# Gated linear attention with a soft mixture of experts on one core: output in 256 and 128 columns, the second expert weights by row halves, one unit in halves

## The chip, the cores and the metric

The kernel runs on one core of a Trainium2 chip. The metric is the device time of one execution in microseconds (us). All data are float32.

## The reference

A gated linear attention runs over 768 steps in 4 × 8 heads of 48 channels. Its output, laid out as x with 3072 rows of 384 columns, goes through a soft mixture of experts: 32 slots, four for each of 8 experts.

```python
f = 1.0 / (1.0 + np.exp(-f_logit))
for t in range(S):
    state = f[:, :, t, :, None] * state + np.einsum('bhd,bhe->bhde', k[:, :, t], v[:, :, t])
    y[:, :, t] = np.einsum('bhd,bhde->bhe', q[:, :, t], state)
...
logits = x @ phi
d = softmax of logits over the rows;  slot_input = d.T @ x
h = np.maximum(slot_input[e] @ w1[e], 0.0);  slot_out[e] = h @ w2[e]
c = softmax of logits over the 32 slots;  out = c @ slot_out
```

The two softmax lines and the two products behind them are written short here; the reference spells them out.

## The kernel before

The sequence is cut into chunks of 128 steps. Twelve units (u = 0 to 11) hold one chunk of two batches each: sixteen heads in eight pairs, 128 partitions by 1024 columns. Pairs 0 to 3 lie in columns 0 to 511, pairs 4 to 7 in the other half.

For each unit ScalarE (ACT) takes exponentials and logarithms of the gates (`d_exp`, `d_ln`), VectorE (DVE) scans them (`d_scan`, L194), ACT forms decay factors (`d_p`, L197, and `d_g`, L203), and GpSimd (POOL) multiplies q and k by them (`d_q`, L211, and `d_k`, L207). TensorE (PE) then computes `scores(u, w)` (L231) for w = 0 (pairs 0 to 3) and w = 1. DVE masks each half (`s_mask`, L240), and since both halves use one PSUM tile, PE may write half 1 only when half 0 is masked. `kt`, `inter`, `kv` and `intra` follow on PE. Units 0 to 2 are processed in two halves of 512 columns each at the start; all others as whole units.

Six groups g of two units each go through the router: logits (`c_lg`), a running maximum over the rows (`c_max`), exponentials (`c_exp`), transposes (`c_tr`, `c_copy`) and a running sum of slot inputs (`c_pin`, `c_join`). `c_max` and `c_join` contain DVE operations on one column (L329, L359).

The order on every engine is that of `at(t, ...)`: each call gets a due time, from a table `OFF` with T = 8.6 for one unit, and the calls are emitted sorted by it. An engine works its instructions off in that order.

After unit 11 comes a list written by hand (`last`, then `tail`). `up` multiplies slot inputs by w1, `turn` transposes the result, `down(h, j, kk)` multiplies by w2 and makes output half h of 192 columns, in 16 steps (j = 0, 1 and kk = 0 to 7). `slot_out` and `slot_out2` scale and spread the sum, `c_soft` and `c_soft2` are the softmax over the slots, `c_ct` transposes its result, and `combine(h, y)` (L486) makes a third y of half h. Copies by ACT (L488) and DVE (L490) put it into a stage in SBUF, and `store` (L493) sends it out: six stores of 768 KB.

All w1 tiles have a home of their own in `wr`. The 16 tiles of w2 (768 KB each, `load_w2`) use space that has been freed: nine go into regions of the arena, the other seven into places of w1 tiles that `up(0, 0)` and `up(0, 1)` have used. A tile holds one expert's 1024 rows by 192 columns, so `down(0, ...)` needs tiles 0 to 7 alone, and the seven late ones are for `down(1, ...)`.

Of the kernel before, what the change touches and what calls it, by code (L numbers as in the profile page):

```python
# [15 lines left out]
L = 128  # L16
NU = 12
# [5 lines left out]
NP = B * H // 2  # L23
NH = 2
HC = DM // NH
# [32 lines left out]
def gla_soft_moe_kernel(ctx: ExitStack, tc: tile.TileContext, q, k, f, v, vd, phi, w1, w2, out):  # L58
# [94 lines left out]
    def warm(n, t=None):  # L153

        for _ in range(n):
            nc.tensor.matmul(PC[:, 1, 384:512] if t is None else t, ones, ones, start=True, stop=True)  # L156

    def consts_1():

        for g in range(4):  # L160
            gs = slice(32 * g, 32 * g + 32)
            nc.vector.tensor_copy(same[gs].rearrange("p (h s) -> p h s", h=4), ident[gs, gs].unsqueeze(1).broadcast_to([32, 4, 32]))

        nc.gpsimd.memset(emask, 0.0)
        for e in range(NE):
            c = 32 * (e // 2) + 4 * e
            nc.gpsimd.memset(emask[:, e % 2, c : c + 4], 1.0)

# [198 lines left out]
    W2 = [(h, 2 * qq + j) for h in range(NH) for j in range(2) for qq in range(4)]  # L367
# [41 lines left out]
    DOWN = [PD[:, 0, :HC], PB[0][:, :HC]]  # L409
    SUM = [PD[:, 1, 256 : 256 + HC], PA[0][:, 256 : 256 + HC]]  # L410
# [13 lines left out]
    def t_zs():  # L424
        nc.vector.tensor_tensor(zs, wb, sms[:, 0:1], op=ALU.mult)
# [8 lines left out]
    ls = el[:, :, 1].rearrange("p v (n s) -> p v n s", n=4)  # L434
    cmv = cm.rearrange("p (v n) -> p v n", v=NV)

    def c_soft():
        cb = cmv.unsqueeze(3).broadcast_to([128, NV, 4, NS])
        nc.vector.tensor_reduce(cmv, ls, axis=AX.X, op=ALU.max)
        nc.vector.tensor_tensor(ls, ls, cb, op=ALU.subtract)  # L440
        nc.scalar.activation(el[:, :, 1], el[:, :, 1], AF.Exp)

    def c_soft2():
        cb = cmv.unsqueeze(3).broadcast_to([128, NV, 4, NS])
        nc.vector.tensor_reduce(cmv, ls, axis=AX.X, op=ALU.add)
        nc.vector.tensor_scalar(cm, cm, 1e-9, None, op0=ALU.add)
        nc.vector.reciprocal(cm, cm)
        nc.vector.tensor_tensor(ls, ls, cb, op=ALU.mult)
# [25 lines left out]
    FIN = [[(PC, PA[0], PA[1]), (PD, PB[1], PA[0]), (PC, PA[1], PB[1])], [(PC, PA[1], PB[1]), (PD, PA[0], PB[0]), (PC, PA[1], PB[1])]]  # L474
    stage = [wr[:, 7 + 3 * h : 10 + 3 * h].rearrange("p a (n d) -> p (a n) d", d=HC).rearrange("p (v n) d -> p v n d", n=4) for h in range(NH)]

    def combine(h, y):

        hs_ = slice(HC * h, HC * h + HC)
        two, b2, b3 = FIN[h][y]  # L480
        banks = [two[:, 0], two[:, 1], b2, b3]
        for n2 in range(2):
            for x in range(2):
                for n in (n2, n2 + 2):
                    ns = slice(32 * n, 32 * n + 32)
# [86 lines left out]
    early = {(1, "kv"): T + 6.0, (3, "scan"): 2 * T + 1.08, (3, "p"): 2 * T + 2.9, (3, "dq"): 2 * T + 2.95}  # L572
# [168 lines left out]
```

## Time and profile before

| | |
|---|---|
| median of 3 runs | 164.55 us (164.38 to 164.94) |
| the profiled execution | 164.74 us, span 163.0 us from first to last instruction |
| mean granted TensorE clock | 0.966 of full speed |
| busy: PE, DVE, ACT, POOL | 143.0, 112.6, 92.6, 53.4 us |
| HBM read, written | 48.82 MB, 4.72 MB |

All times of rows are in us from the start of the span. A row of the timeline has start, duration, engine, line, operation, tiles (out<-in), shape and count; in brackets, if the engine was idle before it, for how long and what released it. A row of the windows has the stretch, its length, busy time and instruction count of PE, PE's weight loads, DVE, ACT and POOL, then the granted TensorE clock (1.00 is 2.4 GHz, 0.50 is 1.2 GHz), the share of the DMA engines' time, and GB/s. The page's slices cut the span into 40 stretches of some 4.1 us and give tenths.

### The profile page before, as it was taken

The page shows a single profiled execution, that of the slowest core. Times are in us where ns is not written, and L with a number is a line of the kernel's source. Part 1 is how long each engine was busy: PE and PEld are TensorE (multiplying, and loading weights), DVE is VectorE, ACT ScalarE, POOL GpSimd, SP SyncE. Part 2 cuts the span into 40 slices and gives each one's busy share as a digit, 9 for nine tenths or more (in the row PEclk, how much of TensorE's full clock was granted, in tenths as well). Part 3 has the DMA queues.
Part 4 walks back from the last instruction along what each step waited for, and adds up shares of the span by engine and source line. Part 5 has one row for each costly group of instructions (what it writes and reads, how often), then busy time and mean ns, then how long its engine had stood idle before and what let it go on. Part 6 is the DMA issues. An engine that isn't in the chain of part 4 may idle for free.

```text
span 163.0 us, 5511 instructions
## 1 busy us (share of the span) xinstructions
PE 143.0 (88%) x2408; PEld 113.6 (70%) x2408; DVE 112.6 (69%) x152; ACT 92.6 (57%) x173; POOL 53.4 (33%) x41
## 2 busy tenths in 40 slices
PE   7998899959999998999989997999989998997500
PEld 7996798949979888798868885867523366664400
DVE  6879998787889979897989888763522708153700
ACT  4977997958778695859596786232302310232500
POOL 2006492665547191908383464600000000000000
PEclk9999999986999999999999999999999999999955
DMA  5999999999999999998999919999947996048690
GB/s 168 286 418 409 409 413 410 405 411 411 400 406 383 385 333 370 410 331 302 339 355 360 339 28 360 414 427 413 417 187 274 414 424 253 0 168 329 261 401 21
DMA packets 13136, 53.97 MB, mean 331 GB/s; under 512 B 1456, under 2 KB 1584, under 8 KB 13104
## 3 DMA queue, kind: packets, MB, share of 16 engines
q1 hardware_dynamic: 13104, 53.55, 84.8%
q8 instruction: 20, 0.33, 0.8%
q14 instruction: 12, 0.10, 0.2%
HBM read 48.82 MB, written 4.72 MB: 328 GB/s over the span
## 4 chain that ended last, share of the span: by engine, by line


## 5 line engine op out<-in xcount | busy, mean ns | idle before, releaser
L211 POOL TENSOR_TENSOR arena<-arena 128x1024 f32<-128x1024 f32 (+1 forms) x11 | 25.0, 2270 | 50.5 <-ACT arena L197 36.1
L240 DVE TENSOR_TENSOR arena<-pd,mask 128x1024 f32<-128x1024 f32 x23 | 27.9, 1213 | 8.7 <-PE pd L231 8.7
L194 DVE TENSOR_TENSOR_SCAN arena<-again,arena 128x1024 f32<-128x1024 f32 (+1 forms) x15 | 30.4, 2036 | 1.7 <-ACT arena L189 1.5
L231 PE MATMUL pd<-arena 48*128 48x128 f32 x368 | 26.7, 285 | 5.2 <-DVE arena L240 3.1
L231 PEld LDWEIGHTS pd<-arena 48*128 48x128 f32 x368 | 22.3, 187 | 9.9 <-DVE arena L240 5.2
L207 POOL TENSOR_TENSOR arena<-arena 128x1024 f32<-128x1024 f32 (+1 forms) x13 | 27.3, 2104 | 0.0
L284 PE MATMUL pb<-arena 128*48 128x128 f32 x384 | 23.5, 274 | 0.8 <-DVE arena L194 0.8
L197 ACT ACTIVATE arena<-arena 128x1024 f32<-128x1024 f32 (+1 forms) x15 | 13.3, 885 | 15.1 <-DVE arena L194 15.1
L284 PEld LDWEIGHTS pb<-arena 128*48 128x48 f32 x384 | 20.4, 123 | 1.5 <-DVE arena L194 1.0
L295 ACT COPY arena<-pb 128x512 f32<-128x512 f32 x24 | 13.5, 586 | 6.5 <-PE pb L284 6.2
L186 ACT ACTIVATE arena<-arena 128x1024 f32<-128x1024 f32 (+1 forms) x15 | 13.3, 887 | 1.7 <-DMA arena<-in_f_dram 1.7
L189 ACT ACTIVATE arena<-arena 128x1024 f32<-128x1024 f32 (+1 forms) x15 | 13.3, 887 | 0.5
L203 ACT ACTIVATE arena<-arena 128x1024 f32<-128x1024 f32 (+1 forms) x15 | 13.4, 893 | 0.3
L300 PE MATMUL pa<-ident,arena 112*128 112x112 f32 x96 | 12.3, 273 | 0.0
L275 PE MATMUL pb<-arena 48*48 48x128 f32 x320 | 10.9, 274 | 0.0
L300 PEld LDWEIGHTS pa<-ident,arena 112*128 112x128 f32 x96 | 10.4, 149 | 0.6 <-issue 0.2
L220 PE MATMUL pc<-ident,arena 112*128 112x112 f32 x80 | 10.6, 280 | 0.0
L156 PE MATMUL pd<-ones 128*128 128x128 f32 x64 | 9.6, 320 | 1.1 <-POOL ones L143 1.1
L156 PEld LDWEIGHTS pd<-ones 128*128 128x128 f32 x64 | 9.2, 233 | 1.2 <-POOL ones L143 1.1
L275 PEld LDWEIGHTS pb<-arena 48*48 48x48 f32 x320 | 8.4, 119 | 2.1 <-issue 1.6
L220 PEld LDWEIGHTS pc<-ident,arena 112*128 112x128 f32 x80 | 8.4, 149 | 1.2
L253 PE MATMUL pc<-arena 128*48 128x48 f32 x320 | 9.2, 210 | 0.0
(137 smaller groups left out, 208.9 us busy)
## 6 DMA issues: line engine op xcount, KB each, us to landing
wr<-in_w_dram SPq DMA_DIRECT2D x23, 768.0 KB, 8.6
arena<-in_w_dram SPq DMA_DIRECT2D x9, 768.0 KB, 9.0
arena<-in_q_dram SPq DMA_DIRECT2D x11, 512.0 KB, 7.5
arena<-in_k_dram SPq DMA_DIRECT2D x11, 512.0 KB, 6.3
arena<-in_f_dram SPq DMA_DIRECT2D x10, 512.0 KB, 7.4
arena<-in_v_dram SPq DMA_DIRECT2D x12, 384.0 KB, 7.1
out_dram<-wr SPq DMA_DIRECT2D x6, 768.0 KB, 3.5
arena<-in_f_dram SPq DMA_DIRECT2D x4, 256.0 KB, 4.0
```

The lines of the kernel that those rows point to most:

```text
L156: nc.tensor.matmul(PC[:, 1, 384:512] if t is None else t, ones, ones, start=True, stop=True)
L194: nc.vector.tensor_tensor_scan(t, cols(again, h), t, 0.0, op0=ALU.mult, op1=ALU.add)
L203: nc.scalar.activation(cols(G(u), h), cols(R("f", u), h), AF.Exp)
L207: (eng or nc.gpsimd).tensor_tensor(t, t, cols(G(u), h), op=ALU.mult)
L211: (eng or nc.gpsimd).tensor_tensor(t, t, cols(R("p", u), h), op=ALU.mult)
L220: nc.tensor.transpose(PC[:, a // 4, 128 * (a % 4) : 128 * (a % 4) + W], kq[:W, a], ident[:W, :W])
L231: nc.tensor.matmul(t[:, 128 * p : 128 * p + 128], kq[rs, 4 * w + p], qq[rs, 4 * w + p], start=True, stop=True)
L240: nc.vector.tensor_tensor(dst, src, mask.unsqueeze(1).broadcast_to(list(dst.shape)), op=ALU.mult)
L275: nc.tensor.matmul(ys[a][o : o + D], heads(S0(u), D)[rs, a], qq[rs, a], start=p == 0, stop=False, skip_group_check=True,)
L284: nc.tensor.matmul(ys[4 * w + p][o : o + D], vb(u, 4 * w + p, r ^ w), sc[:, r, p], start=u < 2 and p == 0, stop=p == 3, skip_group_check=True,
L295: nc.scalar.copy(xTs[u][:, w].rearrange("p a t -> p (a t)"), PB[w])
L300: nc.tensor.transpose(PA[w][:, 128 * p : 128 * p + W], xTs[u][:W, w, p], ident[:W, :W])
```

## The change

Output: instead of two halves of 192 columns there is a part of 256 and a part of 128 (`WC`, `CO`), each stored in three pieces (1024 KB and 512 KB). The tiles of w2 hold 512 rows by all 384 columns, so that both parts use every tile; a tenth tile gets a home in the region `xT`, and six are left for w1's places. Unit 3's `d_scan`, `d_p`, `d_g`, `d_q` and `d_k` run in halves. The softmax over the slots is done by halves of three groups: the first during units 10 and 11, the second in the tail, earlier than before; its two `c_ct` move ahead of the second half of `down(0, ...)`. Three one-column operations become `tensor_scalar` with a scalar per partition. The constants `same` and `emask` are made by POOL at the start instead of by DVE and POOL at 3 T. In `last`, the transposes of unit 11 are split around `c_lg`, and a `warm` gives its place to `c_ct(0)`.

```diff
+WC, CO = (256, 128), (0, 256)
...
-            nc.vector.tensor_tensor(nm(g), nm(g - 1), bmx, op=ALU.min)
+            nc.vector.tensor_scalar(nm(g), bmx, nm(g - 1), None, op0=ALU.min)
...
-            nc.vector.scalar_tensor_tensor(sms[:, 0:1], sms[:, 0:1], alpha, sms[:, 1:2], op0=ALU.mult, op1=ALU.add)
+            nc.vector.tensor_scalar(sms[:, 0:1], sms[:, 0:1], alpha, sms[:, 1:2], op0=ALU.mult, op1=ALU.add)
...
-    W2 = [(h, 2 * qq + j) for h in range(NH) for j in range(2) for qq in range(4)]
+    W2 = [(2 * qq + j, kh) for j in range(2) for kh in range(2) for qq in range(4)]
...
-        t = PA[1] if h else PC[:, 0]
+        t = PA[1] if h else PB[0]
...
-                DOWN[h][32 * qq : 32 * qq + 32], hT[:, j, kk, 32 * qq : 32 * qq + 32], w2u[h, 2 * qq + j][:, kk],
+                DOWN[h][32 * qq : 32 * qq + 32], hT[:, j, kk, 32 * qq : 32 * qq + 32], w2u[2 * qq + j, kk // 4][:, kk % 4, CO[h] : CO[h] + WC[h]],
...
-        items += [(up, 1, 0), (turn, 0, 1), (t_z,), (flag_2,), (up, 1, 1)]
+        items += [(up, 1, 0), (turn, 0, 1), (t_z,), (flag_2,), (c_soft2, 1), (up, 1, 1)]
...
-        items += [(turn, 1, 0), (turn, 1, 1), (c_soft2,)]
-        for x in range(8, 16):
-            items.append((down, 0, *STEPS[x]))
-        items += [(slot_out, 0), (c_ct, 0), (c_ct, 1)]
-        items += [(down, 1, *STEPS[x]) for x in range(2)]
+        items += [(turn, 1, 0), (turn, 1, 1), (c_ct, 1)]
+        items += [(down, 0, *STEPS[x]) for x in range(8, 16)]
+        items += [(slot_out, 0)]
+        items += [(down, 1, *STEPS[x]) for x in range(3)]
         items += [(slot_out2, 0)]
-        items += [(down, 1, *STEPS[x]) for x in range(2, 6)]
+        items += [(down, 1, *STEPS[x]) for x in range(3, 7)]
         for y in range(3):
             items += [(combine, 0, y), (store, 0, y)]
-            items += [(down, 1, *STEPS[x]) for x in ((6, 7, 8, 9), (10, 11, 12, 13), (14, 15))[y]]
+            items += [(down, 1, *STEPS[x]) for x in ((7, 8, 9), (10, 11, 12), (13, 14, 15))[y]]
...
+        (T + 1.08, d_scan, 3, 0), (T + 1.09, d_scan, 3, 1), (T + 2.9, d_p, 3, 0), (T + 2.91, d_g, 3, 0), (T + 2.92, d_q, 3, 0), (T + 2.93, d_k, 3, 0),
+        (T + 2.95, d_p, 3, 1), (T + 2.96, d_g, 3, 1), (T + 2.97, d_q, 3, 1), (T + 2.98, d_k, 3, 1),
...
-    at(3 * T, consts_1)
     at((NU - 1) * T + 6.5, flag)
+    at((NU - 2) * T + 6.45, c_soft, 0)
+    at((NU - 1) * T + 6.4, c_soft2, 0)
...
+    spare = span("xT")[0]
+    homes.append((None, spare))
     late = [(i, wr[:, i - len(homes)]) for i in range(len(homes), 16)]
...
-        (c_lg, NV - 1), (x_tr, NU - 1), (c_max, NV - 1), (c_exp, NV - 1, (0,)), (t_max,), (c_tr, NV - 1, (0,)),
-        (c_copy, NV - 1, (0,)), (x_copy, NU - 1), (t_max2,), (warm, 1), (c_pin, NV - 1), (c_join, NV - 1), (warm, 1),
+        (x_tr, NU - 1, (0,)), (c_lg, NV - 1), (x_tr, NU - 1, (1,)), (load_w2, len(homes) - 1, spare), (x_copy, NU - 1, (0,)), (c_max, NV - 1),
+        (c_exp, NV - 1, (0,)), (x_copy, NU - 1, (1,)), (t_max,), (c_tr, NV - 1, (0,)), (c_copy, NV - 1, (0,)), (t_max2,), (c_ct, 0),
+        (c_pin, NV - 1), (c_join, NV - 1), (warm, 1),
```

## Rows read from the trace of the kernel before

**Rows 1.** The page's 40 slices: DVE, POOL and the granted TensorE clock.
```profile
DVE  6879998787889979897989888763522708153700
POOL 2006492665547191908383464600000000000000
PEclk9999999986999999999999999999999999999955
```

**Rows 2.** Timeline of PE, scores of units 3, 7, 8 and 10.
```profile
34.74 1.16 PE L231 MATMUL pd<-arena 48*128 48x128 f32 x16 [1.83 <-POOL arena L207]
...
39.37 1.16 PE L231 MATMUL pd<-arena 48*128 48x128 f32 x16
...
74.05 1.16 PE L231 MATMUL pd<-arena 48*128 48x128 f32 x16 [0.19 <-DVE arena L240]
...
82.14 1.16 PE L231 MATMUL pd<-arena 48*128 48x128 f32 x16 [0.42 <-DVE arena L240]
...
99.86 1.16 PE L231 MATMUL pd<-arena 48*128 48x128 f32 x16 [1.18 <-DVE arena L240]
```

**Rows 3.** Windows: two stretches around the scores of unit 3.
```profile
32.92:34.74 1.82, 0.00 (x0) 0.00 (x0) 1.40 (x1) 1.80 (x6) 1.82 (x2) 1.00 1.05 423
...
35.92:39.20 3.28, 3.28 (x18) 3.19 (x18) 2.99 (x7) 1.97 (x3) 0.83 (x1) 0.50 1.03 412
```

**Rows 4.** Timelines of DVE, ACT and POOL, 19.8 to 38.9 us.
```profile
20.29 1.21 DVE L194 TENSOR_TENSOR_SCAN arena<-again,arena 128x512 f32<-128x512 f32 x1
...
26.49 2.28 DVE L194 TENSOR_TENSOR_SCAN arena<-again,arena 128x1024 f32<-128x1024 f32 x1
...
33.34 3.49 DVE L194 TENSOR_TENSOR_SCAN arena<-again,arena 128x1024 f32<-128x1024 f32 x1 [0.97 <-ACT arena L189]
36.76 0.89 DVE L162 COPY same<-ident 32x128 f32<-32x128 f32 x4
37.68 1.22 DVE L240 TENSOR_TENSOR arena<-pd,mask 128x1024 f32<-128x1024 f32 x1
...
19.79 0.62 ACT L197 ACTIVATE arena<-arena 128x512 f32<-128x512 f32 x1
...
20.49 2.08 POOL L211 TENSOR_TENSOR arena<-arena 128x512 f32<-128x512 f32 x1 [2.33 <-ACT arena L197]
...
32.33 2.36 POOL L207 TENSOR_TENSOR arena<-arena 128x1024 f32<-128x1024 f32 x1
```

**Rows 5.** Timelines of DVE and POOL in unit 6.
```profile
66.77 0.60 DVE L358 SCALAR_TENSOR_TENSOR pin<-pin,small,pa 128x384 f32<-128x384 f32 x1
67.30 1.93 DVE L359 SCALAR_TENSOR_TENSOR sms<-sms,small 128x1 f32<-128x1 f32 x1
...
66.83 2.38 POOL L207 TENSOR_TENSOR arena<-arena 128x1024 f32<-128x1024 f32 x1
```

**Rows 6.** Timeline of the tail, from the second half of `down(0, ...)`.
```profile
135.72 2.81 PE L458 MATMUL pd<-arena 128*32 128x192 f32 x64 [0.41 <-DVE arena L422]
138.72 0.55 PE L453 MATMUL pc<-ident,el 128*128 128x128 f32 x3 [0.19 <-DVE el L448]
...
142.27 0.42 PE L486 MATMUL pc<-s,ct 32*128 32x192 f32 x1
...
143.24 1.02 DVE L490 COPY wr<-pa 128x384 f32<-128x384 f32 x2 [4.17 <-PE pa L486]
...
144.33 0.35 SPq L493 DMA_DIRECT2D out_dram<-wr  x1
```

**Rows 7.** Windows: end of the late loads, and the stores.
```profile
136.50:137.50 1.00, 1.00 (x32) 0.81 (x28) 0.93 (x3) 0.00 (x0) 0.00 (x0) 1.00 0.43 158
...
145.05:147.00 1.95, 1.95 (x48) 1.23 (x42) 1.02 (x2) 0.80 (x1) 0.00 (x0) 1.00 0.98 403
...
151.75:153.05 1.30, 1.09 (x22) 0.77 (x16) 1.30 (x4) 1.06 (x2) 0.00 (x0) 1.00 0.08 19
...
153.05:159.00 5.95, 0.18 (x5) 0.00 (x0) 1.10 (x3) 0.80 (x1) 0.00 (x0) 0.69 0.98 391
```

More of the change, by code (lines that the diff above doesn't have):

```diff
@@ L23 @@
 NP = B * H // 2
+WC, CO = (256, 128), (0, 256)
 NH = 2
-HC = DM // NH
 UN = 1536
@@ L151, in consts_0 @@
             nc.vector.memset(PB[w], 0.0)
[L153 to L158, printed above, removed]
         for g in range(4):
             gs = slice(32 * g, 32 * g + 32)
-            nc.vector.tensor_copy(same[gs].rearrange("p (h s) -> p h s", h=4), ident[gs, gs].unsqueeze(1).broadcast_to([32, 4, 32]))
+            nc.gpsimd.tensor_copy(same[gs].rearrange("p (h s) -> p h s", h=4), ident[gs, gs].unsqueeze(1).broadcast_to([32, 4, 32]))
         nc.gpsimd.memset(emask, 0.0)
@@ L167, in consts_1, with warm @@
             nc.gpsimd.memset(emask[:, e % 2, c : c + 4], 1.0)
+    def warm(n, t=None):
+        for _ in range(n):
+            nc.tensor.matmul(PC[:, 1, 384:512] if t is None else t, ones, ones, start=True, stop=True)
     def cols(t, h):
@@ L295, in y_copy, with x_tr @@
             nc.scalar.copy(xTs[u][:, w].rearrange("p a t -> p (a t)"), PB[w])
-    def x_tr(u):
-        for w in range(2):
+    def x_tr(u, which=(0, 1)):
+        for w in which:
             for p in range(4):
@@ L424, in t_zs @@
     def t_zs():
-        nc.vector.tensor_tensor(zs, wb, sms[:, 0:1], op=ALU.mult)
+        nc.vector.tensor_scalar(zs, wb, sms[:, 0:1], None, op0=ALU.mult)
     def t_z():
@@ L431, in t_z, with ls, c_soft, c_soft2 @@
         nc.vector.reciprocal(rzs, rzs)
[L434 to L448, printed above, removed]
+    def ls(h):
+        c = cm[:, 12 * h : 12 * h + 12].rearrange("p (v n) -> p v n", v=3)
+        return el[:, 3 * h : 3 * h + 3, 1].rearrange("p v (n s) -> p v n s", n=4), c, c.unsqueeze(3).broadcast_to([128, 3, 4, NS])
+    def c_soft(h):
+        l, c, cb = ls(h)
+        nc.vector.tensor_reduce(c, l, axis=AX.X, op=ALU.max)
+        nc.vector.tensor_tensor(l, l, cb, op=ALU.subtract)
+        nc.scalar.activation(el[:, 3 * h : 3 * h + 3, 1], el[:, 3 * h : 3 * h + 3, 1], AF.Exp)
+    def c_soft2(h):
+        l, c, cb = ls(h)
+        nc.vector.tensor_reduce(c, l, axis=AX.X, op=ALU.add)
+        nc.vector.tensor_scalar(c, c, 1e-9, None, op0=ALU.add)
+        nc.vector.reciprocal(c, c)
+        nc.vector.tensor_tensor(l, l, cb, op=ALU.mult)
     def c_ct(h):
-        t = PA[1] if h else PC[:, 0]
+        t = PA[1] if h else PB[0]
         for x in range(3):
@@ L485, in combine @@
                     ns = slice(32 * n, 32 * n + 32)
-                    nc.tensor.matmul(banks[n][:, HC * x : HC * x + HC], ct[ns, 2 * y + x], s4[ns, hs_], start=True, stop=True)
+                    nc.tensor.matmul(banks[n][:, wc * x : wc * x + wc], ct[ns, 2 * y + x], s4[ns, hs_], start=True, stop=True)
         dst = stage[h][:, 2 * y : 2 * y + 2]
-        nc.scalar.copy(dst[:, :, :2].rearrange("p v n d -> p n v d"), two[:, :, : 2 * HC].rearrange("p n (v d) -> p n v d", v=2))
+        nc.scalar.copy(dst[:, :, :2].rearrange("p v n d -> p n v d"), two[:, :, : 2 * wc].rearrange("p n (v d) -> p n v d", v=2))
         for n in (2, 3):
-            nc.vector.tensor_copy(dst[:, :, n], banks[n][:, : 2 * HC].rearrange("p (v d) -> p v d", v=2))
+            nc.vector.tensor_copy(dst[:, :, n], banks[n][:, : 2 * wc].rearrange("p (v d) -> p v d", v=2))
     def store(h, y):
-        nc.sync.dma_start(out[h][:, 8 * y : 8 * y + 8], stage[h][:, 2 * y : 2 * y + 2].rearrange("p v n d -> p (v n) d"))
+        o, n = 4 * NV * CO[h], 8 * WC[h]
+        nc.sync.dma_start(out[:, o + n * y : o + n * y + n], stage[h][:, 2 * y : 2 * y + 2].rearrange("p v n d -> p (v n d)"))
     gok, gbad = P([128, 2], "gok"), P([1, 1], "gbad", I32)
@@ L582, in gla_soft_moe_kernel @@
         ):
-            if u < 2 and key in done or u == 2 and key in done and key != "pend" or u < 1 and key in done0 or u > NU - 3 and key in ("kt", "ktok", "kv", "st", "s2"):
+            if u < 2 and key in done or u == 2 and key in done and key != "pend" or u == 3 and key in ("scan", "p", "g", "dq", "dk") or u < 1 and key in done0 or u > NU - 3 and key in ("kt", "ktok", "kv", "st", "s2"):
                 continue
@@ L737 @@
     got = r.results[0]["out_0_dram"]
-    got = got.reshape(NH, L, NV, 2, 2, HC).transpose(3, 4, 2, 1, 0, 5).reshape(B * S, DM)
+    got = _np.concatenate([
+        got[:, 4 * NV * o : 4 * NV * (o + n)].reshape(L, NV, 2, 2, n) for o, n in zip(CO, WC)
+    ], axis=-1).transpose(2, 3, 1, 0, 4).reshape(B * S, DM)
     return _np.ascontiguousarray(got)
```

34 lines of the change are left out of this document (19 added, 15 removed).

## The prediction

> **What bounds the kernel now.** I first read the page's slices [rows 1]: the TensorE clock stands at full speed from the start to the end of the computation but for two slices, near 33 to 41 us. So PE does steady work, and it stops once. The timeline of PE shows where [rows 2]: scores(3, 0) start at 34.74 after a wait of 1.83 on POOL. The windows around it [rows 3] show PE at 0.00 busy from 32.92 to 34.74, and then, from 35.92 to 39.20, busy throughout at clock 0.50, the lower of its two levels (1.2 GHz). After that PE waits only now and then, 0.19 to 1.18 us, on masks by DVE [rows 2]. From 20 to 112 us the kernel is therefore a loop PE to DVE to ACT to POOL to PE with PE nearly full, and what makes a unit earlier moves all behind it. The last part has another limit. In its windows [rows 7] the first store's data moves at 403 GB/s, then there is a hole (19 GB/s from 151.75 to 153.05), and the last three stores run at 391 GB/s until 159.0, long after the engines have stopped. So the end is set by when the first store starts and by holes between stores. I read the tail's timeline for that [rows 6].
>
> **Unit 3 in halves.** Now POOL makes q and k of the whole unit, the second product from 32.33 to 34.69, and PE waits for it although scores(3, 0) read only columns 0 to 511 [rows 2, 4]. The scan's first half takes 1.21 as in unit 2 [rows 4], so from 26.49 it ends at 27.70, and the second at about 28.9. ACT's half exponential, 0.62 [rows 4], is done at 28.4. POOL's half product took 2.08 in unit 2, but 20.49 to 21.50 of it lay beside DVE's scan (20.29 + 1.21), so 1.07 without company [rows 4]. I assume that it waits for the second scan half and that four halves of 1.1 follow from 28.9: q at 30.0, k at 31.1, then the other halves, the last at 33.3. PE arrives at 32.92, so scores(3, 0) start at once: the 1.83 is gone, and with it, I assume, the drop of the clock, which cost half of 3.28, or 1.64 [rows 3].
>
> The two do not add up, since DVE is late next. Its scan of unit 4 took 3.49 instead of 2.28: started at 33.34, it got on only when POOL's product ended at 34.69. Then came the copies into `same` (0.89), and only then the mask of scores(3, 0), 37.68 to 38.90; scores(3, 1) run at 39.37 [rows 2, 4]. After the change POOL ends at 33.3, the scan at 33.3 + 2.3 = 35.6, the copies are gone, the mask ends at 36.8, and scores(3, 1) run at 36.9: 2.5 earlier. I take 0.4 off this, because from unit 4 on POOL's products now lie against DVE's scans as they do later, where scores(8, 1) wait 0.42 [rows 2]; before, unit 4 had slack left by the stall. **Term: -2.1.** Bounds: -0.5, if PE stalls and slows as before and only the copies and part of the scan's wait are saved; -2.5 without the deduction.
>
> The copies and fills for `same` and `emask` go to POOL's start. POOL has nothing to do between its first slice and about 12 us [rows 1]; without that cover they would cost some 2 us (0.89 of copies and as much again of fills, as an estimate). Taken as 0.
>
> **Operations on one column.** The update of `sms` took 1.93 us for one element per partition, because it sat until POOL's product ended at 66.83 + 2.38 = 69.21 [rows 5]. Behind it on DVE wait `c_max`, the state update and the scan, and PE's wait of 0.19 for the mask at 74.05 is the only thing that this reaches [rows 2]. The operation before it, with one tensor in SBUF, a scalar per partition and a tensor in PSUM, took its usual 0.60 beside the same product [rows 5], and the new form too reads one tensor and scalars. So the wait goes in units 7 and 9. **Term: 2 × -0.18 = -0.36**, between 0 and -0.8 (if the 0.42 of units 8 and 10 went too). The Trainium skill (SBUF — State Buffer, Who interferes with whom) says that a DVE instruction with two SBUF inputs contends with a POOL instruction that reads SBUF, and one with at most one does not, which these rows bear out. The same section counts `tensor_scalar` among those that may take a mode with both ports and so contend; by that this term would be 0 and the sum 161.4, and no row before shows it.
>
> **Softmax by halves, and the list behind unit 11.** The first half's operations fall in units 10 and 11, where DVE is 30 to 70% busy in slices 26 to 28 [rows 1]. Should they get in the way of a mask, they cost up to 1.5 (four passes over 384 columns at about 0.4). In `last`, `c_ct(0)` takes the place of a `warm`, both about 0.5 on PE, and half of the transposes fill the wait for a copy. I take +0.1 for the list (-0.3 to +0.3). The second half's softmax lies beside `up` and `down`, where DVE has nothing else.
>
> **Output in 256 and 128 columns.** Eight steps of `down(0, ...)` took 2.81 at 192 columns [rows 6]; at 256 they take 2.81 × 4/3 = 3.75, so sixteen steps cost 2 × 0.94 = +1.9. The transposes of `c_ct` (0.55 for the first three, and as much for the other three [rows 6]) stood between `down(0, ...)` and the first combine; one set is now earlier, the other fills the wait of 0.41 ahead of 135.72: -1.0. Ahead of the first combine there were six steps of `down(1, ...)` at 2.81/8 = 0.35, now seven at 0.35 × 2/3 = 0.23: -0.5. Wider scaling and sum: +0.2. So combine(0, 0) moves from 142.27 to 142.9. From there to the first store it was 2.06 (142.27 to 144.33), of which 1.02 are two copies on DVE [rows 6]; with 4/3 of the columns 2.06 becomes 2.5. The first store is 1.1 later, at 145.4, its data from 146.1 instead of 145.05.
>
> In return the holes close. A store of 1.05 MB takes 2.6 us at 403 GB/s, while a combine (1.1) and three narrow steps (0.8) need 1.9: no hole among the first three. They keep the queue busy until 146.1 + 7.8 = 153.9. The first store of part 1 was asked for 5.4 after the start of the third combine (that combine's own copies, the rest of `down`, scaling, sum, combine, copies); now the third combine starts at 146.7, so it is asked for at 152.1, 1.1 us before it would be missed (0.7 go by from request to data). The last two follow each other by about 0.8. Then 4.72 MB move without a hole: 11.7 us at 403 GB/s, to 157.8, against 159.0. At 391 GB/s it would be 12.1 and 158.2. **Term: -1.2**, between +1.1 (holes of 2.3 stay: 13.95 from 145.05 to 159.0, less 11.7) and -1.6. What follows the last data, 159.0 to the end of the span at 163.0, I leave as it is.
>
> **Sum.** -2.1 - 0.36 + 0.1 - 1.2 = -3.6. The profiled execution took 164.74; it becomes 161.2. It lies 0.19 above the median of 164.55, so I forecast 161.0.
>
> **Rivals.** (B) *Unit 3 still stops PE.* The mask ends at 36.8, while PE has done `kt` and two sets of transposes by about 36.0: a new wait of 0.9. If it lowers the clock as the one of 1.82 did [rows 3], 1.6 comes back: 162.6. Against it: the wait of 1.18 at 99.86 [rows 2] is followed by full-speed slices [rows 1].
> (C) *The stores keep their holes* while the first one starts 1.1 later: 164.55 - 2.36 + 1.1 = 163.3. For it: the margin is 1.1 us.
> (D) *The small operations stay held by POOL*, since their scalars too come from SBUF: 161.4.
> (E) *The late w2 tiles come too late, and the kernel is slower.* Before, only part 1 read them. Now the second half of `down(0, ...)` reads six of them, the last four from its fifth step on, at about 136.6 + 1.9 = 138.5. Seven tiles were in at about 137.0, since load traffic falls off after 136.5 [rows 7], each 1.95 at 403 GB/s, so six at 135.1: 3.4 to spare. Each us beyond is lost. From 3.4 + 3.6 = 7.0 us of delay on, it would be slower than before, that is if six tiles took 19 us instead of 12; 165.5 at 8.5.
> (F) *Loads set the pace and the early gain is taken back*: the DMA engines run at shares above 1.00 around unit 3 [rows 3]: 161.0 + 2.1 = 163.1. Against it: PE's waits are on POOL and DVE, none on a load [rows 2].
>
> **How the numbers follow.** As forecast 0.55, B 0.12, C 0.12, D 0.10, E 0.04, F 0.07. D lies inside the likeliest's own range, 160.1 to 161.9. The range from 159.8 to 163.2 takes in B and F and leaves out C and E, 0.16. A change under 0.3% (0.5 us) can't be told from none by this kernel's measurement. All but E, and some mixture of B, C and F (0.04 each for no change and for slower), are faster by more: 0.91, 0.04, 0.05.
>
> **What would show it.** Right: no wait before scores(3, 0), full clock from 33 to 41 us, scores(3, 1) near 37, scores(4, 0) 2 us earlier; the update of `sms` near 0.2; first store 2.4 - 1.1 = 1.3 us earlier in absolute time, and DMA traffic without a hole to the end. Wrong: a second wait in unit 3 with a fall of the clock, a hole ahead of part 1's first store, or a wait of `down(0, ...)` on a load.

## The result, and the profile after

The median is 160.41 us (160.30 to 160.89, four runs) against 164.74 for the kernel before in the same comparison, a ratio of 0.9745 with a 95% interval of 0.9717 to 0.9773. The forecast was 161.0, faster. The profiled execution took 160.30 with a span of 158.6; its mean granted clock is 0.977.

The page's slices of the kernel after, clock and DMA; the slices that stood at 8 and 6 in [rows 1] are full:

```profile
PEclk9999999999999999999999999999999999999955
DMA  4999999999999999998998938999997994009990
```

The timeline of PE, scores of units 3, 4, 7 and 10 (`scores` is L229 now, the mask L238), and then its tail:

```profile
32.79 1.16 PE L229 MATMUL pd<-arena 48*128 48x128 f32 x16
...
37.01 1.16 PE L229 MATMUL pd<-arena 48*128 48x128 f32 x16 [1.15 <-DVE arena L238]
...
41.83 1.16 PE L229 MATMUL pd<-arena 48*128 48x128 f32 x16
...
45.09 1.16 PE L229 MATMUL pd<-arena 48*128 48x128 f32 x16 [0.42 <-DVE arena L238]
...
71.80 1.16 PE L229 MATMUL pd<-arena 48*128 48x128 f32 x16
...
97.16 1.16 PE L229 MATMUL pd<-arena 48*128 48x128 f32 x16 [1.19 <-DVE arena L238]
...
128.83 3.64 PE L458 MATMUL pd<-arena 128*32 128x256 f32 x64
...
133.33 0.49 PE L453 MATMUL pa<-ident,el 128*128 128x128 f32 x3
...
139.75 0.48 PE L490 MATMUL pc<-s,ct 32*128 32x256 f32 x1
```

Against [rows 2], scores(3, 0) no longer wait, but 1.15 us of waiting stand in front of scores(3, 1), on DVE's mask. The 0.19 of unit 7 is gone; the 1.18 of unit 10 is still there.

The timelines of DVE, POOL and SP's queue, with the answers to [rows 4 to 6] (L192 scan, L209 and L205 products, L357 the update of `sms`, L498 the store):

```profile
26.57 2.33 DVE L192 TENSOR_TENSOR_SCAN arena<-again,arena 128x512 f32<-128x512 f32 x2
...
32.69 3.15 DVE L192 TENSOR_TENSOR_SCAN arena<-again,arena 128x1024 f32<-128x1024 f32 x1 [0.38 <-ACT arena L187]
35.76 1.19 DVE L238 TENSOR_TENSOR arena<-pd,mask 128x1024 f32<-128x1024 f32 x1
...
64.79 0.60 DVE L356 SCALAR_TENSOR_TENSOR pin<-pin,small,pa 128x384 f32<-128x384 f32 x1
65.31 0.27 DVE L357 TENSOR_SCALAR sms<-sms,small 128x1 f32<-128x1 f32 x1
...
68.25 2.28 DVE L192 TENSOR_TENSOR_SCAN arena<-again,arena 128x1024 f32<-128x1024 f32 x1
...
140.93 1.29 DVE L494 COPY wr<-pa 128x512 f32<-128x512 f32 x2 [2.88 <-PE pa L490]
...
1.71 1.27 POOL L155 COPY same<-ident 32x128 f32<-32x128 f32 x4
...
28.58 1.39 POOL L209 TENSOR_TENSOR arena<-arena 128x512 f32<-128x512 f32 x1 [3.27 <-ACT arena L195]
...
32.41 1.28 POOL L205 TENSOR_TENSOR arena<-arena 128x512 f32<-128x512 f32 x1
...
64.84 2.37 POOL L205 TENSOR_TENSOR arena<-arena 128x1024 f32<-128x1024 f32 x1
...
142.28 9.44 SPq L498 DMA_DIRECT2D out_dram<-wr  x6
```

The windows around the new wait and over the stores, with the columns of [rows 3] and [rows 7]:

```profile
36.00:37.01 1.01, 0.00 (x0) 0.00 (x0) 1.01 (x2) 1.01 (x2) 0.00 (x0) 1.00 1.00 400
37.10:40.40 3.30, 3.30 (x90) 2.99 (x92) 2.11 (x4) 3.27 (x7) 3.30 (x2) 1.00 1.03 413
...
147.00:149.00 2.00, 1.65 (x43) 1.46 (x47) 1.09 (x4) 1.11 (x3) 0.00 (x0) 1.00 0.98 397
149.00:151.00 2.00, 0.42 (x14) 0.23 (x9) 1.08 (x3) 0.64 (x2) 0.00 (x0) 1.00 1.00 401
...
151.00:154.00 3.00, 0.00 (x0) 0.00 (x0) 0.00 (x0) 0.00 (x0) 0.00 (x0) 0.57 1.01 397
154.00:155.00 1.00, 0.00 (x0) 0.00 (x0) 0.00 (x0) 0.00 (x0) 0.00 (x0) 0.50 0.68 250
155.00:156.50 1.50, 0.00 (x0) 0.00 (x0) 0.00 (x0) 0.00 (x0) 0.00 (x0) 0.50 0.11 44
```

The clock stays at 1.00 behind the wait of 1.15, where [rows 3] had 0.50, and the stores run at about 400 GB/s without the hole of [rows 7].

To see where time went I cut the span at five starts: scores(2, 1), scores(6, 1), scores(10, 1), the first product of `psi` (the first PE work after the router), and the first store. Scores(2, 1) start between 27.06 and 28.32 in these profiles, with no order that follows the edits, so what lies ahead of them is left out of the comparison. (PE stands still there once, for a load in some profiles, 1.74 us up to 13.92 in that of the kernel after, and for DVE in others; the 28.32 is that of e2, where the clock fell behind such a wait.) The segments are differences of starts in the timelines of one profiled execution each, the last one up to the end of the span, in us; two kernels with the same code in a segment agree there within 0.15, but for e5 and e12, which are taken up below. Each ratio is to the kernel before as timed beside that kernel, so ratios, and not medians, compare one row with another. Runs over 1.5% above the fastest of their kernel (166.37 of e11, and some of the kernel before) are left out of the medians and ratios.

| kernel | median | ratio to before, 95% interval | (2,1) to (6,1) | to (10,1) | to psi | to first store | to the end |
|---|---|---|---|---|---|---|---|
| before | 164.74 | | 37.31 | 35.44 | 18.73 | 25.74 | 18.67 |
| after | 160.41 | 0.9745 (0.9717 to 0.9773) | 35.38 | 34.72 | 18.76 | 26.36 | 16.32 |
| e1 unit 3 whole | 162.55 | 0.9863 (0.9821 to 0.9904) | 37.33 | 34.70 | 18.76 | 26.36 | 16.19 |
| e2 small operations as before | 162.12 | 0.9819 (0.9762 to 0.9875) | 35.38 | 35.41 | 19.16 | 26.36 | 16.27 |
| e3 parts of 192 and 192 | 160.86 | 0.9750 (0.9699 to 0.9802) | 35.23 | 34.71 | 18.77 | 24.84 | 18.19 |
| e4 constants late | 162.37 | 0.9828 (0.9780 to 0.9877) | 37.17 | 34.70 | 18.76 | 26.42 | 16.28 |
| e5 before, unit 3 in halves | 165.01 | 0.9987 (0.9961 to 1.0013) | 35.83 | 35.42 | 18.73 | 25.74 | 18.73 |
| e12 the same, second profile | 165.08 (one) | | 37.15 | 35.41 | 18.73 | 25.73 | 18.70 |
| e6 before, PE kept busy | 164.81 | 0.9983 (0.9958 to 1.0008) | 36.90 | 35.45 | 18.74 | 25.74 | 18.69 |
| e7 no tenth home | 161.37 | 0.9778 (0.9740 to 0.9815) | 35.24 | 34.71 | 18.77 | 27.04 | 16.20 |
| e8 softmax late | 161.24 | 0.9758 (0.9718 to 0.9798) | 35.26 | 34.71 | 18.70 | 27.28 | 16.22 |
| e9 two steps fewer | 160.24 | 0.9727 (0.9688 to 0.9767) | 35.26 | 34.73 | 18.75 | 25.93 | 16.24 |
| e10 unit 11 in halves | 161.29 | 0.9803 (0.9778 to 0.9828) | 35.26 | 33.93 | 20.46 | 25.92 | 16.24 |
| e11 units 5, 7, 9, 11 in halves | 163.13 | 0.9916 (0.9892 to 0.9940) | 35.59 | 36.08 | 21.93 | 25.92 | 16.18 |

So the change gave, segment by segment, -1.93, -0.72, +0.03, +0.62 and -2.35, in sum -4.35; the medians differ by 4.33.

### The profile page after: what moved, and what is told of

The parts are those of the page before. It is cut to its first block, busy times and chain, and to the rows that moved or that the text cites. A ratio compares the mean times of both kernels' runs of the same rounds, so it can differ in the third digit from the quotient of the medians.

```text
span 158.6 us, 5522 instructions
## 1 busy us (share of the span) xinstructions
PE 140.2 (88%) x2406; PEld 111.0 (70%) x2406; DVE 107.5 (68%) x155; ACT 93.3 (59%) x176; POOL 54.8 (35%) x47
## 3 DMA queue, kind: packets, MB, share of 16 engines
HBM read 48.82 MB, written 4.72 MB: 338 GB/s over the span
## 4 chain that ended last, share of the span: by engine, by line
## 5 line engine op out<-in xcount | busy, mean ns | idle before, releaser
L209 POOL TENSOR_TENSOR arena<-arena 128x1024 f32<-128x1024 f32 (+1 forms) x12 | 25.1, 2090 | 46.2 <-ACT arena L195 46.2
L238 DVE TENSOR_TENSOR arena<-pd,mask 128x1024 f32<-128x1024 f32 x23 | 27.9, 1213 | 8.7 <-PE pd L229 8.7
L192 DVE TENSOR_TENSOR_SCAN arena<-again,arena 128x512 f32<-128x512 f32 (+1 forms) x16 | 30.2, 1898 | 0.8 <-ACT arena L187 0.7
L229 PE MATMUL pd<-arena 48*128 48x128 f32 x368 | 26.7, 285 | 3.8 <-DVE arena L238 3.8
L229 PEld LDWEIGHTS pd<-arena 48*128 48x128 f32 x368 | 22.3, 187 | 8.2 <-DVE arena L238 5.6
L205 POOL TENSOR_TENSOR arena<-arena 128x1024 f32<-128x1024 f32 (+1 forms) x14 | 27.4, 1966 | 0.0
L195 ACT ACTIVATE arena<-arena 128x512 f32<-128x512 f32 (+1 forms) x16 | 13.5, 841 | 12.1 <-DVE arena L192 12.1
L184 ACT ACTIVATE arena<-arena 128x1024 f32<-128x1024 f32 (+1 forms) x15 | 13.3, 887 | 2.4 <-DMA arena<-in_f_dram 2.4
L201 ACT ACTIVATE arena<-arena 128x512 f32<-128x512 f32 (+1 forms) x16 | 13.6, 850 | 0.3
L187 ACT ACTIVATE arena<-arena 128x1024 f32<-128x1024 f32 (+1 forms) x15 | 13.3, 887 | 0.5
L298 PE MATMUL pa<-ident,arena 112*128 112x112 f32 x96 | 11.6, 262 | 0.0
L298 PEld LDWEIGHTS pa<-ident,arena 112*128 112x128 f32 x96 | 9.7, 141 | 0.7 <-issue 0.2
L218 PE MATMUL pc<-ident,arena 112*128 112x112 f32 x80 | 9.9, 266 | 0.0
L258 DVE TENSOR_TENSOR pc<-pc,arena 128x384 f32<-128x384 f32 x8 | 4.5, 567 | 6.9 <-PE pc L251 6.2
```

The lines of the kernel that those rows point to most:

```text
L192: nc.vector.tensor_tensor_scan(t, cols(again, h), t, 0.0, op0=ALU.mult, op1=ALU.add)
L195: nc.scalar.activation(cols(R("p", u), h), cols(R("f", u), h), AF.Exp, scale=-1.0)
L201: nc.scalar.activation(cols(G(u), h), cols(R("f", u), h), AF.Exp)
L205: (eng or nc.gpsimd).tensor_tensor(t, t, cols(G(u), h), op=ALU.mult)
L209: (eng or nc.gpsimd).tensor_tensor(t, t, cols(R("p", u), h), op=ALU.mult)
L229: nc.tensor.matmul(t[:, 128 * p : 128 * p + 128], kq[rs, 4 * w + p], qq[rs, 4 * w + p], start=True, stop=True)
```

## The experiments

The theory was that of the prediction: unit 3 (stop of PE with a fall of the clock), the two updates that POOL held, and the stores are three separate gains that add up. The rivals were that one part does it all, or that one part costs what another gives. So the first three runs undo one part each.

**e1, unit 3 whole again.**

```diff
-        (T + 1.08, d_scan, 3, 0), (T + 1.09, d_scan, 3, 1), (T + 2.9, d_p, 3, 0), ...
+    early = {(1, "kv"): T + 6.0, (3, "scan"): 2 * T + 1.08, (3, "p"): 2 * T + 2.9, (3, "dq"): 2 * T + 2.95}
```

> The changed kernel with unit 3 whole again, all else as changed. Theory: PE waits for POOL's whole product again, about 1.8 us before scores(3, 0), the clock falls for some 3.4 us, and scores(3, 1) come at about 39.3 instead of 37.0; 2.0 us of it stay at the end, 162.4 us. Rival (the gain of unit 3 came from the constants' copies and the small operations, the halves are worth little): under 0.5 us, 160.9 at most.

Measured: +1.95 in the first segment and nothing elsewhere. PE's timeline and a window of this kernel:

```profile
34.81 1.16 PE L229 MATMUL pd<-arena 48*128 48x128 f32 x16 [1.85 <-POOL arena L205]
```
```profile
36.00:39.30 3.30, 3.30 (x18) 3.17 (x18) 2.13 (x3) 2.00 (x3) 0.86 (x1) 0.50 1.03 411
```

The wait of 1.85 on POOL and 3.3 us at clock 0.50 come back together, as in [rows 2, 3]. Without the halves the first segment's gain is gone.

**e2, the one-column operations in their old form.**

```diff
-            nc.vector.tensor_scalar(nm(g), bmx, nm(g - 1), None, op0=ALU.min)
+            nc.vector.tensor_tensor(nm(g), nm(g - 1), bmx, op=ALU.min)
-            nc.vector.tensor_scalar(sms[:, 0:1], sms[:, 0:1], alpha, sms[:, 1:2], op0=ALU.mult, op1=ALU.add)
+            nc.vector.scalar_tensor_tensor(sms[:, 0:1], sms[:, 0:1], alpha, sms[:, 1:2], op0=ALU.mult, op1=ALU.add)
...
```

> The changed kernel with the three operations on one column in their old forms. The traces of before and after differ by 0.72 us between units 4 and 10, where the prediction had 0.36. Theory: all of it is DVE's hold by POOL, because the scan, and through it the next product on POOL, also start later: the old forms cost 0.7, 161.1 us, the update of sms takes 1.9 again and the scans behind it start 0.35 later in each of units 6 and 8. Rival (the prediction's size, only the wait for the mask): 0.36, 160.8.

Measured: +0.69 in units 6 to 10, and another +0.40 in unit 11. The timeline of DVE in unit 6 of this kernel:

```profile
66.05 0.60 DVE L356 SCALAR_TENSOR_TENSOR pin<-pin,small,pa 128x384 f32<-128x384 f32 x1
66.57 1.91 DVE L357 SCALAR_TENSOR_TENSOR sms<-sms,small 128x1 f32<-128x1 f32 x1
...
69.87 2.28 DVE L192 TENSOR_TENSOR_SCAN arena<-again,arena 128x1024 f32<-128x1024 f32 x1
```

The old form takes 1.91, and the next scan begins 3.82 after the update of `pin`. In the kernel after it is 0.27, and the scan begins 3.46 after (68.25 less 64.79, the start of the same update there). That is 0.36 for each of the two groups in this stretch, together the 0.72. The edit takes back three operations at once; only the update of `sms` is seen held, and whether the one in `c_max` would be held too in the place that it has now is not shown. In unit 11 PE's timeline shows a wait of 0.49 on ACT that the kernel after does not have; the first half of the slots' softmax, which DVE and ACT do there, is queued behind the held operations, which is the likely cause. In this profile the clock also fell to 0.50 at about 14 us, behind a wait of 1.79, which makes the execution longer but lies ahead of the segments.

**e3, two equal parts of the output, all else as changed.**

```diff
-WC, CO = (256, 128), (0, 256)
+WC, CO = (192, 192), (0, 192)
```

(The places of the two stage buffers follow; the hand-written list stays as it is.)

> The changed kernel with two parts of 192 columns, all else as changed. Theory: the first store comes 0.9 to 1.1 us earlier (about 141.3), but a hole of over 1 us stands ahead of the first store of part 1 again, so that the data ends 0.5 to 1.0 us later: 160.9 to 1.4 more, 161.4. Rival (parts don't matter, the stores gained by the earlier softmax alone): the data ends 0.9 us earlier, 159.5.

Measured: the first store 1.52 earlier against psi (24.84 for 26.36), and 1.87 of that given back behind it (18.19 for 16.32). The hole is there again; windows of this kernel:

```profile
148.00:149.50 1.50, 1.29 (x25) 0.80 (x18) 1.50 (x4) 1.18 (x2) 0.00 (x0) 1.00 0.06 16
149.50:152.00 2.50, 0.10 (x1) 0.00 (x0) 1.02 (x3) 0.80 (x1) 0.00 (x0) 1.00 1.02 415
```

So the unequal parts do close the hole, but what they are worth over equal ones is 0.35 in the traces, and the two intervals of the ratios overlap. The list keeps seven steps ahead of the first combine, and equal parts with a list of their own were not tried. With equal parts the first store is still 0.90 earlier than before (24.84 against 25.74), so something else in the tail gained; e8 looks for it.

**e4, the constants late on DVE, as before the change.** The four copies into `same` go back to DVE and 3 T, the fills of `emask` back to POOL and 3 T.

```diff
+    def consts_1():
...
-            nc.gpsimd.tensor_copy(same[gs].rearrange("p (h s) -> p h s", h=4), ident[gs, gs].unsqueeze(1).broadcast_to([32, 4, 32]))
+            nc.vector.tensor_copy(same[gs].rearrange("p (h s) -> p h s", h=4), ident[gs, gs].unsqueeze(1).broadcast_to([32, 4, 32]))
...
+    at(3 * T, consts_1)
```

> The changed kernel with the constants same and emask made at 3 T again, the copies on DVE. Theory: the four copies (0.9 us) stand again between the scan of unit 4 and the mask of scores(3, 0); PE's wait before scores(3, 1) grows from 1.15 to 2.0, so 0.9 is lost, 161.3 us, and if a wait of 2.0 lowers the clock as the one of 1.82 did in the kernel before, up to 1 more, 162.3. Rival (DVE has room there): no change, 160.4.

Measured: +1.79 in the first segment, nearly all that the halves had brought. PE's timeline of this kernel:

```profile
38.44 1.16 PE L231 MATMUL pd<-arena 48*128 48x128 f32 x16 [1.98 <-DVE arena L240]
...
41.92 2.86 PE L284 MATMUL pb<-arena 128*48 128x128 f32 x32
```

0.89 us of copies ahead of the mask make a wait of 1.98 out of 1.15, and behind it the clock falls: `intra` (L284 here) takes 2.86 where it takes 1.92 at full clock. From scores(3, 1) to scores(4, 0) it is 6.28 instead of 4.82, so PE loses 1.46 there to the clock, on top of 0.82 on the way to scores(3, 1); 0.49 of the two is made up before scores(6, 1).

**e5 and e12, the kernel before with nothing but unit 3 in halves.** The diff is that of the change for unit 3 alone. e12 is the same code, profiled once more.

> The kernel before with unit 3 in halves alone. Theory: no wait before scores(3, 0), but the copies of the constants stay on DVE's way to the mask, so scores(3, 1) come at about 37.9 instead of 39.4 and 1.0 to 1.2 us are gained, 163.5; less if the new wait of 2.0 lowers the clock. Rival (the halves alone make the whole gain of unit 3, as the wait and the clock would have it): 2.0 or more, 162.6.

> A second profile of the kernel before with unit 3 in halves. Its first profile kept the full clock after a wait of 1.99 us before scores(3, 1), and the timed gain was 0.2 us where the profile's segment had gained 1.5. Theory (the clock falls after this wait in most executions): this profile shows slices near 0.50 behind the wait, scores(3, 1) to scores(4, 0) takes about 6.3 us and not 4.8, and scores(2, 1) to scores(6, 1) is 36.9 to 37.4 us. Rival (the clock stays, and the gain is lost later): the segment is 35.8 again and the loss is seen behind unit 6.

Measured: in its first profile the segment is 1.48 shorter than before, in the second 0.16. PE's timeline and a window in the first profile (e5):

```profile
38.63 1.16 PE L231 MATMUL pd<-arena 48*128 48x128 f32 x16 [1.99 <-DVE arena L240]
```
```profile
39.50:42.00 2.50, 2.50 (x80) 2.19 (x78) 1.44 (x2) 2.39 (x5) 2.50 (x2) 1.00 1.00 406
```

and in the second (e12):

```profile
38.33 1.16 PE L231 MATMUL pd<-arena 48*128 48x128 f32 x16 [1.96 <-DVE arena L240]
```
```profile
39.50:42.00 2.50, 2.50 (x66) 2.16 (x68) 1.22 (x1) 2.09 (x3) 2.50 (x2) 0.65 1.00 405
```

The wait is nearly the same, the code is the same, and the clock falls in one and stays in the other. Of e5's ten timed runs the profiled one and one more took 164.0 and 163.9 at a mean granted clock of 0.983; the other eight took 164.4 to 165.3 at 0.964 to 0.973. So most executions probably lose what the halves save, as e12 does. This is read from times and clocks together and not shown by traces, since a mean clock alone does not tell it: two runs of the kernel after took 160.40 and 160.41 at 0.969, and the profiled one, without a fall before PE's work ends, took 160.30 at 0.977. The median shows no difference from before that can be measured. Halves without the moved constants gain nothing in the median, and (e4) they lose nearly all of their gain when the constants go back: the gain belongs to the pair. The traces also divide the cost of the constants: with the clock up they cost 0.45 of the segment (35.83 in e5, 35.38 in the kernel after), and the fall of the clock adds 1.3 (37.15 in e12).

**e6, the kernel before, with PE kept busy through its wait.** Seven products of ones, with a result that nothing reads, fill the stop of [rows 2].

```diff
+    at(3 * T - 0.01, warm, 7)
```

> The kernel before with seven matmuls of ones (1.7 us of PE work whose result nobody reads) put into PE's wait ahead of scores(3, 0). Theory: the clock stays at 1.00, scores(3, 0) come at 34.8 as before, and since DVE's scan, copies and mask end at 38.9 whatever PE does, scores(3, 1) gain only 0.4 us: 164.3. Rival (the half clock itself was the loss): 1.6 us, 163.1.

PE's timeline of this kernel:

```profile
33.31 1.83 PE L156 MATMUL pc<-ones 128*128 128x128 f32 x14
35.21 1.16 PE L231 MATMUL pd<-arena 48*128 48x128 f32 x16
...
39.43 1.16 PE L231 MATMUL pd<-arena 48*128 48x128 f32 x16 [1.15 <-DVE arena L240]
```

The clock stays at full, and the segment gains 0.41; then PE waits 1.15 for a mask that comes no earlier than before. So the fall of the clock cost the loop 0.4 and not the 1.64 that PE lost by itself: DVE was the next one late, as the prediction had assumed when it did not add the two. The gain is the trace's; the interval of the ratio takes in 1.

**e7, the tenth home taken away,** so that seven tiles of w2 are late and not six.

```diff
-    homes.append((None, spare))
...
-    assert len(late) <= 6
+    assert len(late) <= 7
```

> The changed kernel without the tenth early home of a w2 tile: seven tiles are loaded late into the places of w1 tiles, as before the change. Theory: the last late tile lands some 1.9 us later than now, still ahead of the fifth step of the second half of down(0, ...) at about 134.7, or at most 1 us behind it: 160.4 to 161.4. Rival (the tenth home is what makes the row halves possible): the tile is over 1.5 us late, 161.9 or more.

Measured: +0.68 before the first store. The timeline of PE's weight loads (PEld) and two windows of this kernel (L458 is `down`):

```profile
136.62 1.22 PEld L458 LDWEIGHTS pd<-wr,arena 128*32 128x32 f32 x25 [0.57 <-DMA wr<-in_w_dram]
```
```profile
134.00:135.00 1.00, 0.98 (x18) 0.55 (x20) 0.72 (x2) 0.48 (x1) 0.00 (x0) 1.00 0.77 320
135.00:136.00 1.00, 1.00 (x27) 0.58 (x18) 0.00 (x0) 0.00 (x0) 0.00 (x0) 1.00 0.20 61
```

`down(0, ...)` waits 0.57 for the last tile, which lands at 136.6 (issued at 123.3, landed 13.3 later); in the kernel after the last tile lands at 134.4 (122.5 and 11.9). Counted from psi the tile is 1.9 later here, as the theory had it, and that costs 0.68, so the changed kernel has some 1.2 to spare, where rival E had counted 3.4. The windows show why E counted too much: it took the end of the load traffic for the arrival, but traffic falls off about 2 us before the last tile has landed, here at some 134.7, in the kernel after at 132.4.

**e8, the softmax over the slots in one piece's place again,** that is both halves in the tail and `c_ct` between `down(0, ...)` and the first combine.

```diff
-        items += [(turn, 1, 0), (turn, 1, 1), (c_ct, 1)]
+        items += [(turn, 1, 0), (turn, 1, 1), (c_soft2, 0), (c_soft2, 1)]
...
-        items += [(slot_out, 0)]
+        items += [(slot_out, 0), (c_ct, 0), (c_ct, 1)]
...
-    at((NU - 2) * T + 6.45, c_soft, 0)
-    at((NU - 1) * T + 6.4, c_soft2, 0)
```

> The changed kernel with both halves of the softmax over the slots and both sets of transposes back in their places in the tail, after down(0, ...). Theory: PE does six transposes between down(0, ...) and the first combine, so the first store and all that follow come 0.6 to 1.0 us later, 161.0 to 161.4. Rival (that work lies in waits anyway): no change, 160.4.

Measured: +0.92 before the first store, nothing elsewhere. PE's timeline of this kernel:

```profile
134.12 0.41 PE L458 MATMUL pd<-arena 128*32 128x256 f32 x2 [0.35 <-DVE arena L420]
...
137.71 0.55 PE L453 MATMUL pc<-ident,el 128*128 128x128 f32 x3
138.10 0.49 PE L453 MATMUL pa<-ident,el 128*128 128x128 f32 x3
...
140.95 0.48 PE L490 MATMUL pc<-s,ct 32*128 32x256 f32 x1
```

Both sets of transposes stand between the last step of part 0 and the narrow steps, and the wait ahead of the second half of `down(0, ...)` (0.35 at 134.12), which one of them fills at 133.33 in the kernel after, is idle. The earlier softmax and `c_ct` are thus what gained in the tail beside the closed hole. e3 had kept a like amount, 0.90, but the match is partly chance, since its list also has a seventh step of some 0.35 ahead of the first combine. The gain is the trace's: the ratios, 0.9758 and 0.9745, differ by only 0.2 us, and their intervals overlap.

**e9, two steps of `down(1, ...)` fewer ahead of the first combine.** A version that could beat the changed kernel.

```diff
-        items += [(down, 1, *STEPS[x]) for x in range(3, 7)]
+        items += [(down, 1, *STEPS[x]) for x in range(3, 5)]
...
-            items += [(down, 1, *STEPS[x]) for x in ((7, 8, 9), (10, 11, 12), (13, 14, 15))[y]]
+            items += [(down, 1, *STEPS[x]) for x in ((5, 6, 7, 8), (9, 10, 11, 12), (13, 14, 15))[y]]
```

> The changed kernel with two narrow steps of down(1) fewer ahead of combine(0, 0); each of them takes about 0.23 us. Theory (the first store waits for PE's list, and the stores then run without a hole to the end): combine(0, 0) and the first store are 0.4 to 0.45 us earlier, no hole appears because the third combine's data is still asked for before the second store is through, and the time is about 160.0 us. Rival (the steps filled a wait for slot_out2's sum): combine(0, 0) waits for DVE in their place, the first store is where it was, and the time stays at 160.4.

Measured: the first store is 0.43 earlier against psi, and the end follows it (16.24). The median is 160.24; the interval of its ratio overlaps that of the kernel after, so the trace shows the gain and the times do not yet prove it.

**e10, unit 11 in halves as well (on top of e9), with the scan asked for behind the mask of scores(10, 0).**

```diff
+    HV = (3, 11)
+    for u in HV:
+        for t, fn, *args in (
+            (1.08, d_scan, u, 0), (1.09, d_scan, u, 1), (2.9, d_p, u, 0), (2.91, d_g, u, 0), ...
+        ):
+            at((u - 1) * T + t, fn, *args)
```

> As the kernel with two steps fewer, and unit 11 is treated as unit 3: scan, decay factors and products in two halves, with the first half of the scan asked for after the mask of scores(10, 0) and not before it. Theory (a unit's wait for a mask is DVE being held in a scan beside POOL's products): the wait of 1.19 us before scores(10, 1) goes, and psi and all behind it is 0.9 to 1.2 us earlier, so about 159.1 us. Rival (the scan is on the loop that sets the pace): scores(11, 0) then wait for POOL instead, and nothing is gained, 160.0.

Measured: the time rises, from 160.24 in e9 to 161.29. PE's and DVE's timelines of this kernel:

```profile
96.88 1.16 PE L229 MATMUL pd<-arena 48*128 48x128 f32 x16 [0.41 <-DVE arena L238]
99.57 0.85 PE L352 MATMUL pa<-arena,el 128*32 128x384 f32 x8 [1.53 <-DVE arena L303]
...
96.74 2.33 DVE L192 TENSOR_TENSOR_SCAN arena<-again,arena 128x512 f32<-128x512 f32 x2
98.99 0.53 DVE L303 COPY arena<-pa 128x384 f32<-128x384 f32 x1
```

The wait before scores(10, 1) shrinks from 1.18 to 0.41 as the theory said, but the next products wait 1.53: the copy of unit 10's transposes (L303) is queued on DVE behind the scan, and `c_pin` (L352) needs it. In e9 the scan came first, at 94.01, and this copy ran at 97.65. Theory and rival both missed: it was neither gain nor POOL, but a queue.

**e11, units 5, 7, 9 and 11 in halves (on top of e9).**

```diff
-    HV = (3, 11)
+    HV = (3, 5, 7, 9, 11)
```

> As the one with unit 11 in halves, and units 5, 7 and 9 in halves too. Theory: the waits of 0.42 us before the second scores of units 4, 6 and 8 go as well, up to 1.2 us, about 157.9. Rival: four half products on POOL take 5.16 us (4 x 1.29) where two whole ones take 4.74, the scan of the next unit comes later by it, and the loop gains nothing or loses up to 0.4 per unit: 159.1 to 160.3.

Measured: 163.13, and in the profiled execution (164.99) nearly all of the change's gain is gone. PE's timeline and a window of this kernel:

```profile
47.32 0.85 PE L352 MATMUL pa<-arena,el 128*32 128x384 f32 x8 [1.24 <-DVE arena L303]
...
101.87 1.51 PE L352 MATMUL pa<-arena,el 128*32 128x384 f32 x8 [1.53 <-DVE arena L303]
```
```profile
102.50:105.00 2.50, 2.50 (x41) 1.58 (x33) 1.25 (x3) 0.41 (x2) 2.50 (x3) 0.52 1.04 423
```

Every even unit changes a wait of 0.42 for one of 1.24, and here the clock falls behind the wait of 1.53 that left it alone in e10. The timed runs lie in two groups, 162.8 to 163.1 at a mean clock of 0.979 to 0.981, and 165.0 to 165.3 at 0.968; the profile is of the second, and that the first is without the fall is not shown. A list in which the copy goes ahead of the scan was not tried.

## Why the prediction was right

In sum the change gave 4.35 where the prediction's sum had 3.6: the mechanisms were right, and two of its four terms were too small.

**Unit 3 (-2.1, measured -1.93).** Each step is in the trace: no wait at scores(3, 0), scores(3, 1) at 37.01 (forecast 36.9), scores(4, 0) at 41.83 instead of 44.09. The deduction of 0.4 was right as well: 2.36 are gained up to scores(3, 1), and 0.43 of them are lost again by scores(6, 1), with a wait of 0.42 before scores(4, 1) that the kernel before did not have. Two details were off and cancel by luck: POOL ends at 33.7 (32.41 + 1.28) and not 33.3, since its four halves take 1.28 to 1.39 and not 1.1, and DVE's next scan takes 3.15 and not 2.3, but starts at 32.69 and not behind POOL, so that it ends at 35.84 (forecast 35.6). Rival B's wait was nearly right in size (0.9 forecast, 1.15 measured) and its other half did not come: the clock stayed at 1.00, as behind the 1.18 of [rows 2]. Behind the longer waits of e4 and e12 (1.98 and 1.96) it did come, behind that of e5 (1.99) it did not. The constants were rightly costed at nothing: POOL copies them from 1.71 on and then stands idle until 13.59. Without that cover they cost 1.79 (e4); the estimate was some 2 us, but it is near by luck, since it added copies and fills, and most of the 1.79 is the fall of the clock.

**Operations on one column (-0.36, measured -0.72): the mis-sized term.** The cause was right, as e2 shows. The size was taken from the one wait that PE showed, 0.19 for a mask. But DVE stood 0.36 late with its scan too, and the scan sets exponential, products and the scores after next; what reached PE in the later units is not marked there as a wait on these operations. The right number for each was the 0.36 by which the next scan on the same engine was late. The bounds, 0 to -0.8, held it. Rival D fell with this: the update takes 0.27 while POOL's product runs (64.84 to 67.21). The Trainium skill (SBUF — State Buffer, Who interferes with whom) counts `tensor_scalar` among the operations that can take both ports and contend, when their operands meet its conditions; this form, one element per partition with two scalars from SBUF, was not held.

**List behind unit 11 (+0.1, measured +0.03).** Right. e2 adds that with the old operations this stretch cost 0.40 more, probably because the first half of the softmax is hidden there only as long as DVE isn't held.

**Output (-1.2, measured -1.73): right in kind, mis-sized at one step.** "combine(0, 0) moves from 142.27 to 142.9" was the step: +0.6, measured +0.15 (from 23.68 behind psi, 142.27 less 118.59, to 23.83, 139.75 less 115.92). e8, which has the wide parts in the old order of `c_ct`, divides it: its first combine is 24.75 behind psi (140.95 less 116.20), so the wide and narrow steps with scaling and sum cost +1.07 where the sum had 1.9 - 0.5 + 0.2 = 1.6, and the earlier `c_ct` gives 0.92 where it had 1.0. The two sets of eight wide steps were too dear in it. The whole 2.81 was scaled by 4/3 to 3.75, and the set takes 3.64; and the second set absorbed the 0.19 for which PE had waited ahead of `c_ct` [rows 6]. From psi to the second set e8 is 0.79 behind before (17.92 against 17.13), over the second set 0.59 (3.59 against 3.00), and from there to the combine 0.31 ahead, where the sum had 0.3. From combine to store the kernel after takes 2.53, forecast 2.5, and the closed hole gave 2.35, forecast 2.3 (13.95 less 11.7). Rival C, holes that stay, fell. What the prediction did not see is how the gain divides: the 256 and 128 columns by themselves are worth only 0.35 over equal parts (e3), because they delay the first store by 1.52 for the 1.87 that the hole gives back.

**Rivals E and F.** No transfer took the early gain back. E's margin exists, but is 1.2 and not 3.4, because the last tile lands some 2 us after the traffic falls off (e7). Two side sums of the prediction don't come out: 8.5 us of delay would give 161.0 + 8.5 - 3.4 = 166.1 and not 165.5, and 0.91 for faster leaves too little for E at 0.04 and two mixtures at 0.04 each. The forecast rests on neither.

## What to carry to other kernels

When a wait is removed from a loop, look at which engine's operation is late next, and clear that in the same edit: halves alone (the median of e5) and constants alone (the first segment of e1) were each worth nothing, together 1.9 us. Size a held operation by how much later the next loop operation on its own engine starts, not by the wait that another engine happens to show. Before an instruction is moved behind another in an engine's queue, list what is already queued between them: the halves that gained in unit 3 lost in units 5 to 11, because a copy that PE needed had come to stand behind them.

## What the runs showed of the hardware that was not expected

The clock after a wait of one length is not fixed. Behind waits of 1.79 to 1.98 us it fell to 0.50 in the profiles of before, e1, e2, e4 and e12; behind 1.99 in e5 and 1.74 in the kernel after it stayed at 1.00; around a wait of 1.53 it fell in e11 and stayed in e10; behind those of 1.0 to 1.43 it stayed in every profile. A fall cost PE about 1.5 us (4.72 from scores(3, 1) to scores(4, 0) in e5, 6.27 in e12). What of it reached the loop depends on who is late next: 0.4 in the kernel before (e6), 1.3 in e12 against e5. A kernel that waits 2 us on PE once can so have two times about 1 us apart. The Trainium skill (TensorE: Matmul & The Clock Gate, What's actually happening) says of the start of a kernel that the number of slow products varies from run to run; these runs show that a fall behind a wait in the middle varies too.

The end of load traffic is not the arrival of the data: the last w2 tile landed some 2 us after the traffic fell off (134.4 against 132.4 in the kernel after, 136.6 against some 134.7 in e7).
